# A decode layer with a sliding attention window: one more 64 KB transfer from ScalarE's queue

## The chip, the cores and the metric

The kernel runs on one core of a Trainium2 chip. The metric is the time of one execution in microseconds (us) on the device; lower is better. The time before is 377.72 us, the median of 3 runs (377.6 to 378.23).

A core has five engines with instruction streams of their own: PE (matrix products), DVE and ACT (vector and scalar work), POOL, and SP, which in this kernel only issues transfers. Transfers are carried out by 16 DMA engines, which the queues of SP and ACT share.

## The reference

One decode step (one token for each of 4 sequences) of a transformer layer, in bfloat16: attention over the last 4096 entries of a key-value cache, then a gated feed-forward.

```python
B, Sq, D = 4, 1, 576
Hq, Hkv, Sk, Dh = 32, 16, 16384, 128
W = min(4096, max(256, Sk // 4))                 # 4096
q = (layernorm(x) @ wq)                          # [4, 32 heads, 1, 128]
k = repeat(k_cache[:, :, Sk - W:, :], 2, axis=1) # two query heads share a key head
v = repeat(v_cache[:, :, Sk - W:, :], 2, axis=1)
p = softmax(q k^T * Dh ** -0.5)
h = x + (p v) @ wo
gate, up = layernorm(h) @ W_gate, layernorm(h) @ W_up
out = h + (relu(gate) * up) @ W_down             # F = 4608
```

The keys and values of the window are 2 x 64 MiB, the weights some 25 MB; nothing is used twice from HBM.

## The kernel before

**Order by hand.** A small class `Sched` writes each engine's program one after the other. `S.op` adds an instruction, `S.dma` a transfer; both take a list of names to wait for (`deps`) and may give a name that others wait for. Every engine has one counting semaphore, every key of transfers one of its own, and a wait is a wait on constants. The order in a program is the order on its engine. A transfer counts 16 on its semaphore when it is through; `land(name)` is the name under which its landing is waited for.

**The loads.** `prog_sync` issues all loads but one from SP's queue, in this order: wq's last 64 rows (`("wq", 4)`, 512 KB), its first 512 rows (`("wq", 0)`, 4 MB), then K and V. The attention goes over 16 quads, one for four key heads of one sequence: `quad(cache, i)` gives the window of four heads as 128 partitions (32 to a head) with 32768 contiguous bytes each, 4 MB in all. K0, K1, V0, K2, V1, ... alternate over a pool of four slots in SBUF; each issue waits until the reader of the slot's old content is through (`("TR", ...)` for a K slot, `("PV", i)` for a V slot, `"QMM"` for the two slots that wq lies in at first). Then follow wo, W_gate, W_up and, in six pieces of falling size (`WD`, line 253), W_down. The only other load is x (four rows of 1152 bytes), from ScalarE's queue, line 291.

**The products with wq.** wq's 512 first rows are read as 128 partitions of four rows each and are multiplied with `xnT`, the transposed normalised x. The 64 last rows are read as 128 half rows, and are multiplied with `xn4`, in which each value of x stands on two partitions and `par` keeps the one or the other (lines 307 to 309): the odd products. PE takes these first (`c == 4`, line 483), since their load lands first; they wait for `"XN41"`, the second of the two xn4 copies. The last product is `"QMM"`. After it ACT copies q to `q_bf` (line 311), DVE transposes it into `qT` (line 427, after the first transpose of K0), and PE spreads it (`"QREP"`).

**The attention.** For each quad, four times: DVE transposes a quarter of K in 32-bit units into `kT` (`tr`, line 395; `kT` has NKT = 3 buffers of 2048 float32 on each partition, used in turn), and PE multiplies it with the spread q (`qk`, line 497). The maximum, exponentials, a transpose of the probabilities and the products with V (`pv`, line 515) follow, V of a quad one quad behind its K.

**The end.** wo, the second layer norm, the gated products and W_down, whose pieces PE takes in order as they land; the last product is `"DOWN1"`, after which ACT and DVE copy one part of the output each and SP stores it.

ACT's program around the change, in order: x is issued; small constants; `D_X4`, `D_XNT` (the transposed x from PSUM); `FOE`, `IDF`, `SPOT`, `SAME` (line 305); the two copies `XN40` and `XN41`; the copies of q.

Of the kernel before, what the change touches and what calls it, by code (L numbers as in the profile page):

```python
# [9 lines left out]
BF16 = mybir.dt.bfloat16  # L10
# [91 lines left out]
def bass_sequential_preLN__sliding_block_cached__glu_gated_reglu__decode_kernel(  # L102
# [12 lines left out]
    with ExitStack() as es:  # L115
        cnt = [0]

        def sb(name, shape, dt):
            return es.enter_context(nc.sbuf_tensor(name, shape, dt))

        pool = sb("pool", [128, NSLOT * QUAD], BF16)
        kT = sb("kT", [128, NKT, QUAD // 8], FP32)
# [74 lines left out]
        S = Sched()  # L197
# [56 lines left out]
        for k, (f0, f1) in enumerate(WD):  # L254
            transfers.append((("wd", k), f"wd{k}", ["ATTN"],
                              lambda e, f0=f0, f1=f1: e.dma_start(
                                  out=pool[:, f0 * D:f1 * D], in_=B_W_down.rearrange("(p j) n -> p (j n)", j=JJ)[:, f0 * D:f1 * D])))
# [4 lines left out]
        def land(name):  # L262
            return ("L",) + (name if isinstance(name, tuple) else (name,))
# [25 lines left out]
        def prog_act(S):  # L289
            a = "scalar"  # L290
            S.dma(a, lambda e: e.dma_start(out=x_bf[:, :], in_=A_x.rearrange("b s d -> (b s) d")), "x", name=land("x"))
            S.op(a, lambda e: e.activation(out=st1[:, 14:15], in_=st1[:, 13:14], func=ACT.Sqrt, bias=eps_c[0:B, 0:1], scale=1.0),
                 deps=["D_VAR", "EPS"], name="A_STD")
            S.op(a, lambda e: e.copy(out=dup[:, :].rearrange("p (r u) -> p r u", u=2),
                                     in_=bass.AP(tensor=ident_b, offset=0, ap=[[128, 64], [1, 64], [0, 2]])), deps=["IDB"], name="DUP")
            S.op(a, lambda e: e.copy(out=col[:, :].rearrange("p (a s) -> p a s", s=NS),
                                     in_=bass.AP(tensor=ident_b, offset=0, ap=[[128, NS], [0, 128], [1, NS]])), name="COL")
# [3 lines left out]
                                           in_=bass.AP(tensor=ident_b, offset=0, ap=[[128, NS], [0, 16], [1, NS], [0, 2]]),  # L301
# [2 lines left out]
            S.op(a, lambda e: e.activation(out=spot[:, :], in_=spot[:, :], func=ACT.Copy, scale=-SCALE), deps=["SPOT0"], name="SPOT")  # L304
            S.op(a, lambda e: e.copy(out=same[:, :].rearrange("p (x h) -> p x h", h=NHQ),
                                     in_=bass.AP(tensor=mask, offset=0, ap=[[NHQ, 128], [0, 16], [1, NHQ]])), deps=["M0"], name="SAME")
            for u in range(2):
                S.op(a, lambda e, u=u: e.activation(out=xn4[:, u, 0:B], in_=pb[STB][:, 0:B], func=ACT.Copy, scale=par[:, u:u + 1]),
                     deps=["XDUP", "PAR2", "XN4Z"], name=f"XN4{u}")
            for k in range(2):  # L310
                S.op(a, lambda e, k=k: e.copy(out=q_bf[:, k, :].rearrange("p (x e k) -> p x e k", e=2, k=32),
                                              in_=pb[QB[k]].rearrange("p (x k e) -> p x e k", e=2, k=32)), deps=["QMM"], name=f"QBF{k}")
            S.op(a, lambda e: e.copy(out=qrep[:, :, :].rearrange("p x (g y) -> p x g y", g=4),
                                     in_=sc.ap().rearrange("p (g r) -> p g r", g=4)[:, :, 0:128].rearrange("p g (x y) -> p x g y", x=4)),
                 deps=["QREP"], name="D_QR")
# [16 lines left out]
            for i in range(NQUAD):  # L332
                S.op(a, lambda e, i=i: e.activation(out=diag[:, i % 2, :], in_=spot[:, :], func=ACT.Copy, scale=rmx[:, i % 2:i % 2 + 1]),  # L333
                     deps=[("RMAX", i), "SPOT"], name=("DIAG", i))
                deps = [("BIAS", i)]
                if i >= 2:
                    deps.append(("TRP", i - 2))
                S.op(a, lambda e, i=i: e.activation(  # L338
                    out=Pb[:, (i % 2) * 1024:(i % 2 + 1) * 1024], in_=sc[:, (i % 2) * 1024:(i % 2 + 1) * 1024], func=ACT.Exp,
                    scale=SCALE, bias=bias[:, i % 2:i % 2 + 1], accum_out=rs1[:, i:i + 1]),  # L340
                    deps=deps, name=("EXP", i))
                if i + 2 < NQUAD:
                    qzero(i + 2)
            S.op(a, lambda e: e.copy(out=bass.AP(tensor=spread, offset=0, ap=[[16 * H, H], [4 * H + 1, 4], [4, H]]),
                                     in_=bass.AP(tensor=ident_b, offset=0, ap=[[128, H], [0, 4], [1, H]])),
                 deps=["SP0"], name="SPREAD")
            S.op(a, lambda e: e.copy(out=oX[:, :, :].rearrange("p e b -> p (e b)"), in_=pb[0][:, 0:EO * B]), deps=["OSEL"], name="OX")  # L347
            S.op(a, lambda e: e.activation(out=st2[:, 14:15], in_=st2[:, 13:14], func=ACT.Sqrt, bias=eps_c[0:B, 0:1], scale=1.0),
                 deps=["D_VAR2"], name="A_STD2")
            S.op(a, lambda e: e.copy(out=hnT[0:64, 4, 0:B], in_=tpv[0:64, 16:20]), deps=["TP2", "HN4Z"], name="N1")  # L350
            S.op(a, lambda e: e.copy(out=hnT[:, 0:4, 0:B], in_=tpv[:, 0:16].rearrange("p (c b) -> p c b", b=B)), name="N2")
            for u in range(2):
                S.op(a, lambda e, u=u: e.activation(out=hn4[:, u, 0:B], in_=pb[SUB][:, 400:400 + B], func=ACT.Copy, scale=par[:, u:u + 1]),
                     deps=["HDUP"], name=f"HN4{u}")
            for k, (f0, f1) in enumerate(CUTS):
                S.op(a, lambda e, k=k, f0=f0, f1=f1: e.activation(out=gate_sb[:, :, f0:f1].rearrange("p j f -> p f j"), in_=part(0, k, "f j"), func=ACT.Relu),
                     deps=[("GATE", k)], name=("RELU", k))
# [3 lines left out]
        def prog_dve(S):  # L361
# [12 lines left out]
            for k in range(5):  # L374
                w = 1 << k
                S.op(v, lambda e, w=w: e.tensor_scalar(out=num[:, w:2 * w], in0=num[:, 0:w], scalar1=float(w), scalar2=None, op0=ALU.add),
                     deps=["NUM0"] if k == 0 else [("NUM", k - 1)], name=("NUM", k))
            S.op(v, lambda e: e.transpose(out=numT[:, :], in_=num[:, :]), deps=[("NUM", 4)], name="NUMT")
            for k in range(4):
                S.op(v, lambda e, k=k: e.tensor_tensor(out=ident_b[32 * k:32 * k + 32, 32 * k:32 * k + 32], in0=num[32 * k:32 * k + 32, :],  # L380
                                                       in1=numT[32 * k:32 * k + 32, :], op=ALU.is_equal),
                     deps=["NUMT", "P0"] if k == 0 else [], name="IDB" if k == 3 else None, signal=k == 3)
# [4 lines left out]
                 name="PAR2")  # L387
# [6 lines left out]

            def tr(i, j):
                f = 4 * i + j
                deps = [land(("K", i))]
                if f >= NKT:
                    deps.append(("QK", f - NKT))
                x0 = at[("K", i)] + j * (QUAD // 4)  # L400
                src = pool[:, x0:x0 + QUAD // 4].bitcast(FP32).rearrange("p (t c k) -> p c t k", c=2, k=32)
                dst = kT[:, f % NKT, :].rearrange("p (c t k) -> p c t k", c=2, k=32)
                S.op(v, lambda e: e.transpose(out=dst, in_=src), deps=deps, name=("TR", f))  # L403
# [19 lines left out]
            for i in range(NQUAD):  # L423
                for j in range(4):
                    tr(i, j)
                    if i == 0 and j == 0:
                        S.op(v, lambda e: e.transpose(out=qT[:, :], in_=q_bf[:, :, :].rearrange("p k x -> p (k x)")), deps=["QBF1"], name="D_QT")  # L427
                        S.op(v, lambda e: e.tensor_reduce(out=bass.AP(tensor=gath, offset=0, ap=[[2 * H, 128], [H + 16, 2], [NHQ, 2], [1, NHQ]]),
                                                          in_=bass.AP(tensor=ident_f, offset=0, ap=[[128, 128], [0, 2], [64, 2], [1, NHQ], [NHQ, 8]]),
                                                          axis=AX.X, op=ALU.add), deps=["IDF", "G0"], name="GATH")  # L430
                    if j == 0 and i > 1 and i % 2 == VLEAD:
                        own(i // 2 - 1)
                rmax(i)
                fbias(i)
                trp(i)
# [8 lines left out]
                 deps=["RS", ("EXT", NQUAD // 2 - 1)], name="NORM")  # L444
# [3 lines left out]
            for k, (f0, f1) in enumerate(CUTS):  # L448
                S.op(v, lambda e, k=k, f0=f0, f1=f1: e.tensor_tensor(out=hh[:, :, f0:f1], in0=part(1, k, "j f"), in1=gate_sb[:, :, f0:f1], op=ALU.mult),
                     deps=[("GU", k), ("RELU", k)], name=("HH", k))  # L450
            for j in range(2):
                j0, j1 = j * JJ // 2, (j + 1) * JJ // 2
                S.op(v, lambda e, j0=j0, j1=j1: e.transpose(out=hhT[:, j0:j1, :].rearrange("p j b -> p (j b)"),
                                                            in_=hh[:, j0:j1, :].rearrange("p j f -> p (j f)")),
                     deps=[("HH", len(CUTS) - 1)], name=("HHT", j))
# [3 lines left out]
        def prog_pe(S):  # L459
# [134 lines left out]
            for k, (f0, f1) in enumerate(WD):  # L594
                deps = [land(("wd", k))]
                for f in range(f0, f1):
                    if f % (JJ // 2) == 0:
                        deps = deps + [("HHT", f // (JJ // 2))]
                    for u in range(2):
# [3 lines left out]
                        deps = []  # L603

        progs = [("gpsimd", prog_pool), ("sync", prog_sync), ("scalar", prog_act), ("vector", prog_dve), ("tensor", prog_pe)]
        S.begin(False)
        for _, p in progs:
# [32 lines left out]
```

## Time and profile before

| what | value |
|---|---|
| median of 3 runs | 377.72 us (377.6 to 378.23) |
| the profiled execution | 378.56 us |
| its span, first to last instruction | 377.2 us |
| busy: PE, DVE, ACT, POOL | 80%, 60%, 14%, 1% |
| packets of queue q1 (SP) | 159.59 MB, 98.8% of 16 DMA engines' span |
| K load, issue to landing (median of 16) | 26.8 us |
| V load, issue to landing (median of 16) | 26.4 us |
| chain that ended last | DMA 47%, DVE 29%, PE 20%, ACT 3% |

A busy share is that of one engine over the span. The chain that ended last is followed back from the last instruction, at each step to what released it. A line of a timeline has the start in us, the duration in us, the engine, the line in the code, the operation, what it writes and reads, and in brackets how long the engine had been idle and what ended that. A line of the table of stretches has the stretch, its length, then busy time and (x) instructions of PE, PEld (weight loads), DVE, ACT and POOL, the granted clock of PE, the DMA share and GB/s.

These are the issues from SP's queue that the prediction speaks of, and three around them, from the timeline of that queue:

```profile
1.64 1.25 SPq L226 DMA_DIRECT2D pool<-in_A_k_cache_dram  x2
17.55 0.54 SPq L231 DMA_DIRECT2D pool<-in_A_v_cache_dram  x1
18.13 0.60 SPq L226 DMA_DIRECT2D pool<-in_A_k_cache_dram  x1
...
319.43 0.33 SPq L245 DMA_DIRECT2D pool<-in_A_wo_dram  x1
...
352.45 2.70 SPq L256 DMA_DIRECT2D pool<-in_B_W_down_dram  x6
```

K0 and K1 are issued at 1.64 us, V0 and K2 when wq's slots are free at 17.55, and the six pieces of W_down at 352.45.

### The profile page before, as it was taken

What the parts mean: (1) busy time and instruction counts of PE and PEld (TensorE: products, weight loads), DVE (VectorE), ACT (ScalarE), POOL (GpSimd) and SP (SyncE); (2) the same over time, 40 slices, a digit from 0 to 9 for tenths busy, and PEclk for the clock granted to TensorE, in tenths of its full rate; (3) what the DMA queues carried; (4) which work ended last, traced back from release to release, by engine and by line L of the source; (5) the groups of instructions that cost most, each with busy time, mean ns of one, the idle gap of its engine ahead of it and who ended that gap; (6) DMA issues with size and microseconds to landing.
All of it is one profiled execution on the core that took longest, in us unless ns stands there. A gap on an engine that the chain in (4) does not pass through costs nothing.

```text
span 377.2 us, 2603 instructions
## 1 busy us (share of the span) xinstructions
PE 302.2 (80%) x1432; PEld 73.0 (19%) x772; DVE 225.8 (60%) x165; ACT 53.4 (14%) x140; POOL 5.2 (1%) x15
## 2 busy tenths in 40 slices
PE   0509299969996999499969996899879996968667
PEld 0101022212221222022212221122112121212214
DVE  8046677595849493858476846666675768231230
ACT  2202402110220112002200220020202010101020
POOL 5000000000000000000000000000000000000000
PEclk9999789998999899989989997799959998996988
DMA  8999999999999999999999999999999999999996
GB/s 334 445 445 389 445 440 393 445 440 438 422 424 441 438 434 408 441 441 427 413 440 441 431 427 427 440 434 427 420 441 440 417 424 441 422 432 429 443 404 255
DMA packets 6506, 159.74 MB, mean 423 GB/s; under 512 B 728, under 2 KB 864, under 8 KB 1632
## 3 DMA queue, kind: packets, MB, share of 16 engines
q1 hardware_dynamic: 6488, 159.59, 98.8%
q8 instruction: 8, 0.13, 0.1%
q10 hardware_dynamic: 8, 0.00, 0.0%
q14 instruction: 2, 0.02, 0.0%
HBM read 159.58 MB, written 0.00 MB: 423 GB/s over the span
## 4 chain that ended last, share of the span: by engine, by line
DMA 47%; DVE 29%; PE 20%; ACT 3%; SPq 1%; issue 1%; DVEq 0%
DMA pool<-in_A_k_cache_dram 41%; DVE kT L403 20%; PE sc L466 7%; PE sc L468 6%; DMA pool<-in_B_W_down_dram 5%; DVE acc L420 4%; PE val L466 3%; PE val L468 3%; DVE own_sb L417 2%; DVE probT L414 2%; ACT P L338 2%; PE pb L466 1%; DVE o_bf L442 0%; ACT L338 0%; DVE rmx L406 0%
## 5 line engine op out<-in xcount | busy, mean ns | idle before, releaser
L403 DVE STREAM_TRANSPOSE kT<-pool 128x2048 f32<-128x2048 f32 x64 | 142.8, 2278 | 25.3 <-DMA pool<-in_A_k_cache_dram 24.3
L466 PE MATMUL sc<-kT,qz 128*128 128x512 bf16 x256 | 110.5, 432 | 36.6 <-DVE kT L403 36.3
L468 PE MATMUL sc<-kT,qz 128*128 128x512 bf16 x256 | 109.6, 428 | 0.0
L466 PE MATMUL val<-pool,probT 128*64 128x512 bf16 (+2 forms) x328 | 104.2, 374 | 4.4 <-DMA pool<-in_B_W_down_dram 4.4
L468 PE MATMUL val<-pool,probT 128*64 128x512 bf16 x256 | 96.2, 379 | 0.0
L466 PEld LDWEIGHTS sc<-kT,qz 128*128 128x128 bf16 x256 | 26.7, 104 | 146.5 <-issue 71.1
L466 PEld LDWEIGHTS val<-pool,probT 128*64 128x64 bf16 (+1 forms) x328 | 32.1, 107 | 81.3 <-issue 68.5
L406 DVE TENSOR_REDUCE rmx<-sc 128x1 f32<-128x1024 f32 x16 | 19.6, 1225 | 41.0 <-PE sc L468 41.0
L333 ACT ACTIVATE diag<-spot,rmx 128x16 f32<-128x16 f32 x16 | 4.9, 307 | 234.0 <-DVE rmx L406 234.0
L414 DVE STREAM_TRANSPOSE probT<-P 128x1024 bf16<-128x1024 bf16 x16 | 19.9, 1246 | 21.0 <-ACT P L338 21.0
L338 ACT ACTIVATE P<-sc,bias 128x1024 bf16<-128x1024 f32 x16 | 17.8, 1114 | 21.0 <-DVE bias L409 21.0
L327 ACT COPY qz<-qrep 32x128 bf16<-32x128 bf16 x64 | 18.8, 294 | 0.6
L409 DVE TENSOR_REDUCE bias<-pb 128x1 f32<-128x16 f32 x16 | 2.8, 175 | 23.8 <-PE pb L466 23.8
L420 DVE TENSOR_REDUCE acc<-own_sb 128x128 f32<-128x1024 f32 x8 | 15.2, 1897 | 0.3
L417 DVE TENSOR_TENSOR own_sb<-val,mask 128x1024 f32<-128x1024 f32 x8 | 9.6, 1200 | 7.9 <-PE val L468 7.9
L466 PE MATMUL sc<-pool,oX 128*4 128x288 bf16 x32 | 10.0, 338 | 0.4 <-ACT oX L347 0.4
L468 PE MATMUL sc<-pool,oX 128*4 128x288 bf16 x32 | 9.9, 336 | 0.0
L478 PE MATMUL pb<-ident_b,xn_bf 4*128 4x4 bf16 (+1 forms) x5 | 0.4, 180 | 10.0 <-DVE xn_bf L371 10.0
L466 PE MATMUL sc<-qT,sel 32*128 32x128 bf16 x4 | 0.3, 284 | 9.6 <-DVE qT L427 9.6
L445 DVE TENSOR_TENSOR h_row<-sc,x_bf 4x576 f32<-4x576 f32 x1 | 0.7, 745 | 11.6 <-PE sc L468 11.6
L466 PE MATMUL pb<-diag,same 128*128 128x16 f32 x32 | 6.3, 273 | 1.7 <-ACT diag L333 1.7
L466 PEld LDWEIGHTS pb<-diag,same 128*128 128x128 f32 x32 | 4.8, 188 | 11.8 <-ACT diag L333 7.4
(102 smaller groups left out, 85.7 us busy)
## 6 DMA issues: line engine op xcount, KB each, us to landing
pool<-in_A_k_cache_dram SPq DMA_DIRECT2D x16, 4096.0 KB, 26.8
pool<-in_A_v_cache_dram SPq DMA_DIRECT2D x16, 4096.0 KB, 26.4
pool<-in_A_wo_dram SPq DMA_DIRECT2D x1, 4608.0 KB, 18.3
pool<-in_B_W_gate_dram SPq DMA_DIRECT2D x1, 4608.0 KB, 18.6
pool<-in_B_W_up_dram SPq DMA_DIRECT2D x1, 4608.0 KB, 24.7
pool<-in_A_wq_dram SPq DMA_DIRECT2D x1, 4096.0 KB, 12.7
pool<-in_B_W_down_dram SPq DMA_DIRECT2D x1, 2016.0 KB, 15.0
pool<-in_B_W_down_dram SPq DMA_DIRECT2D x1, 1296.0 KB, 17.7
```

Source lines behind the costliest of these rows:

```text
L327: S.op(a, lambda e, src=src, dst=dst: e.copy(out=dst, in_=src), deps=deps, name=("QZ", i) if g == 3 else None, signal=g == 3)
L333: S.op(a, lambda e, i=i: e.activation(out=diag[:, i % 2, :], in_=spot[:, :], func=ACT.Copy, scale=rmx[:, i % 2:i % 2 + 1]), deps=[("RMAX", ...
L338: S.op(a, lambda e, i=i: e.activation(out=Pb[:, (i % 2) * 1024:(i % 2 + 1) * 1024], in_=sc[:, (i % 2) * 1024:(i % 2 + 1) * 1024], func=ACT ...
L403: S.op(v, lambda e: e.transpose(out=dst, in_=src), deps=deps, name=("TR", f))
L406: S.op(v, lambda e: e.tensor_reduce(out=rmx[:, i % 2:i % 2 + 1], in_=sc[:, (i % 2) * 1024:(i % 2 + 1) * 1024], axis=AX.X, op=ALU.max), dep ...
L409: S.op(v, lambda e: e.tensor_reduce(out=bias[:, i % 2:i % 2 + 1], in_=pb[TPB][:, 16 * (i % 2):16 * (i % 2) + 16], axis=AX.X, op=ALU.min), ...
L414: S.op(v, lambda e: e.transpose(out=pT[i % NPT], in_=Pb[:, (i % 2) * 1024:(i % 2 + 1) * 1024]), deps=[("EXP", i)] + ([("PV", i - NPT)] if ...
L417: S.op(v, lambda e: e.tensor_tensor(out=own_sb[:, :].rearrange("p (x d) -> p x d", d=DH), in0=val[:, :].rearrange("p (x d) -> p x d", d=DH ...
L420: S.op(v, lambda e: e.tensor_reduce(out=acc[:, w % 2, :], in_=own_sb[:, :].rearrange("p (x d) -> p d x", d=DH), axis=AX.X, op=ALU.add), de ...
L445: S.op(v, lambda e: e.tensor_tensor(out=h_row[:, :], in0=attn, in1=x_bf[:, :], op=ALU.add), deps=["ATTN", land("x")], name="H")
L466: return e.matmul(o, lhsT=l, rhs=r, start=start, stop=stop, skip_group_check=skip)
L468: return e.add_instruction(mybir.InstMatmult(name=nc.get_next_instruction_name(), start_tensor_calc=start, stop_tensor_calc=stop, bass_ski ...
```

## The change

ScalarE issues one more transfer, after `SAME` and ahead of the two xn4 copies. It reads the first eight rows of wq as four pieces of two rows (16384 contiguous bytes each) and writes them to partitions 0, 8, 16 and 24 of the first two buffers of `kT`, which nothing has used by then. Nothing reads them. Since DVE's first transpose overwrites the first buffer, it waits for this transfer to land as well as for K0. Everything else stays.

```diff
             S.op(a, lambda e: e.copy(out=same[:, :].rearrange("p (x h) -> p x h", h=NHQ),
                                      in_=bass.AP(tensor=mask, offset=0, ap=[[NHQ, 128], [0, 16], [1, NHQ]])), deps=["M0"], name="SAME")
+            S.dma("scalar", lambda e: e.dma_start(
+                out=kT[0:32:8, 0:2, :].rearrange("p f n -> p (f n)").bitcast(BF16), in_=A_wq[0:8, :].rearrange("(a c) n -> a (c n)", c=2)),
+                "stagger", name=land("stagger"))
             for u in range(2):
                 S.op(a, lambda e, u=u: e.activation(out=xn4[:, u, 0:B], in_=pb[STB][:, 0:B], func=ACT.Copy, scale=par[:, u:u + 1]),
                      deps=["XDUP", "PAR2", "XN4Z"], name=f"XN4{u}")
@@
             def tr(i, j):
                 f = 4 * i + j
-                deps = [land(("K", i))]
+                deps = [land(("K", i))] + ([land("stagger")] if f == 0 else [])
                 if f >= NKT:
                     deps.append(("QK", f - NKT))
```

## Prediction

> **What bounds the kernel now.** I read first the page's DMA rows, then busy time in four stretches, then the end of the timeline, and last the trace's record of every DMA packet (start, duration, bytes, queue, but no engine number).
>
> ```profile
> span 377.2 us, 2603 instructions
> ...
> DMA  8999999999999999999999999999999999999996
> ...
> q1 hardware_dynamic: 6488, 159.59, 98.8%
> q8 instruction: 8, 0.13, 0.1%
> q10 hardware_dynamic: 8, 0.00, 0.0%
> q14 instruction: 2, 0.02, 0.0%
> ```
>
> The 16 DMA engines are busy from end to end: SP's queue q1 alone fills 98.8% of them. PE (80%) and DVE (60%) follow what lands. q10 is ScalarE's queue; its 8 packets are the four rows of x and four semaphore writes, so a transfer with four outer rows runs on four engines. q8 fetches instructions in 8 packets of 16384 bytes.
>
> ```profile
> 3.60:20.00 16.40, 5.27 (x46) 1.18 (x26) 6.03 (x19) 3.29 (x13) 2.11 (x6) 1.00 0.98 422
> 20.00:57.00 37.00, 22.23 (x83) 4.67 (x45) 23.29 (x14) 7.14 (x18) 0.00 (x0) 0.91 1.01 425
> 62.00:97.00 35.00, 31.53 (x133) 7.33 (x69) 24.49 (x16) 5.17 (x14) 0.00 (x0) 0.95 1.00 433
> 101.00:320.00 219.00, 191.19 (x777) 43.40 (x403) 149.39 (x92) 27.36 (x73) 0.00 (x0) 0.92 1.00 432
> ```
>
> The last column is GB/s. Between 20 and 57 us the queues are full and yet move 425 GB/s, later 433. (The first stretch has smaller packets and bins that cut them, so it is not compared.)
>
> ```profile
> 374.00 1.38 PE L466 MATMUL val<-pool,probT 128*4 128x320 bf16 x14 [0.39 <-DMA pool<-in_B_W_down_dram]
> ...
> 375.42 0.41 ACT L358 CAST out_sb<-val 4x320 bf16<-4x320 f32 x1 [13.51 <-PE val L466]
> 375.42 0.42 DVE L456 CAST out_sb<-val 4x256 bf16<-4x256 f32 x1 [9.02 <-PE val L466]
> 375.91 0.33 SPq L269 DMA_DIRECT2D out_dram<-out_sb  x1
> ```
>
> The end hangs on the last piece of W_down: PE waits for it, then about 2.5 us of fixed tail follow. A transfer has landed when the slowest of its 16 engines is through, so the time is set by **the engine that is last at 374.7 us**.
>
> The packet records give that engine. On one engine each packet starts 3 ns before the one before it ends, so the packets link into 16 chains of 405 (45 loads, 8 data packets and a semaphore write each); which chain is which engine the records don't say. A 32768-byte packet takes 1213 ns when undisturbed. Three findings:
> - From 20 to 57 us the mean is 1241 ns, with all chains within 0.4 us of one another and slowed in the same rounds: 479 packets, 0.84 us per engine. From 62 to 97 us the mean is 1215.5 ns. The slowing stops at 57 us, where the first instruction fetch (56.58 us) throws one chain 1.6 us behind the other fifteen.
> - Each of the 8 fetches hits another chain, which stays behind: 1.53 to 1.65 us at the end for seven, 1.96 us for one that was 0.4 us late already. Two more chains, hit by q14's two 8192-byte packets, are 0.63 and 0.93 us behind; six are within 0.28.
> - The chain ahead of all ends at 372.73 us, the last at 374.69, and PE goes on at 374.72.
>
> **The change, part by part.**
>
> ```profile
> 11.10 0.28 ACT L305 COPY same<-mask 128x128 f32<-128x128 f32 x1
> 11.29 0.40 ACT L308 ACTIVATE xn<-sc,par 128x4 bf16<-128x4 f32 x2
> ...
> 13.89 0.62 PE L466 MATMUL val<-pool,xnT 128*32 128x512 bf16 x4 [1.02 <-DMA pool<-in_A_wq_dram]
> ```
>
> *The issue.* One transfer more in ScalarE's queue, between these two ACT rows; the issue of x took 0.55 us there. That moves the two xn copies, and PE's eight odd-product matmuls with them, by at most 0.55 us; they end 1.02 us before wq lands, so half the cover is left. Without cover it would still cost nothing: the q copies end at 18.63 us and the transpose that reads them starts at 25.88. What is queued behind the issue on ACT (q copies, qrep, qz) waits for PE anyway.
>
> *The wait.* The first K transpose (23.64 us) also waits for the new transfer. Issued at 11.4 us, it should land by 16 at the latest (x took 1.2 us from issue to its last row; here a packet of up to 1.4 us stands ahead on each engine). Nothing; behind it on DVE stands all of the attention, which would move by what is late.
>
> *The bytes.* 16384 bytes on each of four engines that are never idle. Nothing later gives that time back: each of these engines runs every following packet later by s. Lower bound of s: half a 32768-byte packet, 0.61 us. Upper bound: the fetches, packets of the same size from another queue, which cost their chains 1.4 to 1.7 us each. The 8192-byte ones cost 0.58 and 0.85 us where their bytes alone would be 0.30, so a change of queue takes 0.28 to 0.55 us on top. 0.61 plus 0.4 is **s = 1.0 us**, taken nearer the plain packets, since it too is an HBM-to-SBUF copy.
>
> Where s shows at the end depends on which chains it falls on. On a chain that no fetch hits (0 to 0.94 us behind), it ends 1.0 to 1.94 behind, not later than today's last: **0**. On one that is hit (1.55 to 1.65), it ends about 2.6 us behind, 0.65 us later than today's last (bounds: 0.2 to 1.4). Following the two late rows of x through the first 2 us, the closest links lead to chains without a fetch, or to a tie between one with and one without, so I lean to the first.
>
> *The rounds between 20 and 57 us.* s comes at about 12.5 us, before they begin, and puts four chains where one chain was put at 57 us. If being in step is the cause, the 0.84 us go, all but the 0.07 or so that the stretch from 62 to 97 us also shows: **-0.75 us** for every chain. Bounds: 0 (the stretch slows for another reason) and -1.1 (the one chain that is 0.4 us late by then is spared too). A loss is bounded by the last rival.
>
> *What is issued earlier or later.* Landings of K move by -0.75 to +1.0 us, and the loads that wait for freed slots move with them. By the packet records a load's first packet starts 5.2 us after its issue at least (wo: issued 319.43, started 324.61), so no engine runs dry.
>
> [...]
>
> **Sum.** 0 (issue) + 0 (wait) + 0 (s on chains with room) - 0.75 (rounds). The profiled execution took 378.56 us, 1.3 more than its span of 377.2; the median of the runs is 377.72, and I put the difference on that: **377.0 us**.
>
> **Rivals.**
> - *Rounds gone, but s falls on a chain that a fetch hits later.* -0.75 + 0.65 = -0.1: 377.6 us. For it: eight of sixteen chains are hit. Against it: the links of x.
> - *In step is not the cause, and s has room.* 377.7 us: a transfer wholly hidden. For it: the slowing began at 20 us in the middle of a load, though the chains had been in step since 13. Against it: its end falls on the very packet at which the first fetch strikes.
> - *In step is not the cause, and s falls on a hit chain.* +0.65: 378.4 us. This is plain added work on a full engine.
> - *The slowing lasts longer.* One mechanism on the other side: the shift is close to a whole packet (1.21 us), so the four chains fall into the same rhythm one packet later, and the fetch at 57 us, which can strike one of these four or leave too many in step, no longer ends the rounds. They would then go on to the next fetch at 97.7 us: 41 us at 0.84 per 37 is +0.9, and with half of the 0.65 for a hit chain +1.2: 378.9 us. It decides if more than about 15 us of further rounds are added. Against it: one chain 1.6 us off was enough before.
> - *It doesn't do what it says* (the pieces spread over 16 engines): 64 KB over 16 is 0.15 us each and no stagger, within the second rival; x's four rows on q10 speak against it.
>
> **Chances.** Forecast 0.44, rivals in order 0.18, 0.06, 0.20, 0.12. About 0.2%, 0.76 us, is what a measurement of this kernel can tell from no change. The forecast sits on that edge: 0.32 of its 0.44 counts as faster, since what can be spared reaches to -1.1, and 0.12 as no change. The first rival gives 0.03, 0.14 and 0.01; the second 0.06 no change; the third 0.06 no change and 0.14 slower; the fourth 0.12 slower. Together faster 0.35, same 0.38, slower 0.27. The range runs from 376.4 (all of the bound -1.1, and the runs' own spread below the median) to 378.9 (the fourth rival). The forecast's own range is 376.4 to 377.4.
>
> **What would show it.** In the changed profile: 20 to 57 us at 432 or 433 GB/s (rounds gone) or at 425 (not); four chains 0.6 to 1.5 us behind from 13 us on; q10 with 16 packets (right) or 40 (spread); the largest lag at the end 1.6 to 1.9 us (room) or 2.2 to 3.3 (hit); K0's first transpose at most 1 us later; wq's products starting up to 1 us later without effect on V0's landing. The prediction fails if the rounds stay, if they last past 57 us, or if s lies far above 1.5 us.

## The result and the profile after

The changed kernel takes 378.4 us (median of 22 runs, 377.95 to 378.58), the kernel before 377.75 us in as many runs beside it (377.56 to 378.42): ratio 1.0015 with a 95% interval of 1.0008 to 1.0021, **0.65 us slower**. 377.0 us was forecast, with 376.4 to 378.9 as the range.

The profiled execution of the changed kernel took 378.58 us. The page's lines on the DMA engines:

```profile
span 377.2 us, 2605 instructions
...
DMA  8999999999999999999999999999999999999995
...
q1 hardware_dynamic: 6488, 159.59, 98.6%
q8 instruction: 8, 0.13, 0.1%
q10 hardware_dynamic: 16, 0.07, 0.0%
q14 instruction: 3, 0.02, 0.0%
```

The span is that of before to the tenth, and ScalarE's queue q10 has the 16 packets that four pieces on four engines give (e6_eight's eight pieces make 24 of them, e4_sixteen's 16 pieces 40; q14's third packet has 80 bytes). The four stretches (busy time of PE, PEld, DVE, ACT, POOL, granted clock, DMA share, GB/s):

```profile
3.60:20.00 16.40, 5.27 (x46) 1.20 (x26) 6.03 (x19) 3.29 (x13) 2.11 (x6) 1.00 0.99 418
20.00:57.00 37.00, 20.98 (x75) 4.20 (x41) 22.07 (x13) 6.84 (x17) 0.00 (x0) 0.72 1.00 429
62.00:97.00 35.00, 31.53 (x132) 7.34 (x69) 25.09 (x16) 3.62 (x10) 0.00 (x0) 0.95 0.99 426
101.00:320.00 219.00, 191.46 (x784) 43.67 (x408) 151.19 (x93) 27.34 (x73) 0.00 (x0) 0.93 1.00 431
```

From 20 to 57 us the rate rose from 425 to 429 GB/s, but from 62 to 97 us it fell from 433 to 426, though the packet records show nothing there: a 32768-byte packet took 1217 ns on average in the first of these stretches and 1219.9 from 57 to 97 us. A packet counts in GB/s where it falls, so the column is good to some 4 GB/s over 35 us (an estimate: four 32768-byte packets more or fewer), and the packet records are the sharper reading. They say that the rounds of 20 to 57 us are gone (1241 ns before).

Timelines: first around the new issue, then the ends.

```profile
10.47 0.68 ACTq L307 DMA_DIRECT2D kT<-in_A_wq_dram  x1
...
11.28 0.40 ACT L311 ACTIVATE xn<-sc,par 128x4 bf16<-128x4 f32 x2
...
14.03 0.62 PE L469 MATMUL val<-pool,xnT 128*32 128x512 bf16 x4 [1.16 <-DMA pool<-in_A_wq_dram]
...
17.69 0.54 SPq L231 DMA_DIRECT2D pool<-in_A_v_cache_dram  x1
...
24.87 2.31 DVE L406 STREAM_TRANSPOSE kT<-pool 128x2048 f32<-128x2048 f32 x1 [14.93 <-DMA pool<-in_A_k_cache_dram]
```

```profile
374.74 0.09 PEld L469 LDWEIGHTS val<-pool,probT 128*4 128x4 bf16 x4 [0.33 <-DMA pool<-in_B_W_down_dram]
...
375.44 0.41 ACT L361 CAST out_sb<-val 4x320 bf16<-4x320 f32 x1 [13.65 <-PE val L469]
375.44 0.42 DVE L459 CAST out_sb<-val 4x256 bf16<-4x256 f32 x1 [8.84 <-PE val L469]
375.93 0.34 SPq L269 DMA_DIRECT2D out_dram<-out_sb  x1
```

ACT's sequencer issues the transfer at 10.47 us, while the engine still works on what stands ahead of it (`SAME` starts at 11.09), and the xn copies stay where they were (11.28, before 11.29). wq's products come 0.14 us later and V0's issue too; K0's first transpose comes 1.23 us later (before 23.64). The end is the same as in the profile of before (375.93, before 375.91), and PE waits for W_down as before.

So the two *profiled* executions are equal, and the *medians* are 0.65 us apart. The packet records, linked into 16 chains as in the prediction, show how (the chains are a reconstruction: where two end within a few ns of one another, a link can be exchanged):

| | before | after |
|---|---|---|
| the chain ahead of all ends at | 372.73 us | 372.04 us |
| the last chain ends at | 374.69 us | 374.68 us |
| lag of the last | 1.96 us | 2.65 us |

The chain ahead gained 0.69 us, and one chain took 0.69 us back. The experiments had to tell which of the two belongs to the median.

### The profile page after: what moved, and what is told of

The parts are those of the page before. It is cut to its first block, busy times and chain, and to the rows that moved or that the text cites. A ratio compares the mean times of both kernels' runs of the same rounds, so it can differ in the third digit from the quotient of the medians.

```text
span 377.2 us, 2605 instructions
## 1 busy us (share of the span) xinstructions
PE 301.3 (80%) x1432; PEld 73.2 (19%) x772; DVE 225.7 (60%) x165; ACT 53.4 (14%) x140; POOL 5.2 (1%) x15
## 3 DMA queue, kind: packets, MB, share of 16 engines
q1 hardware_dynamic: 6488, 159.59, 98.6%
## 4 chain that ended last, share of the span: by engine, by line
DMA 45%; DVE 29%; PE 21%; ACT 3%; issue 0%; SPq 0%; DVEq 0%
DMA pool<-in_A_k_cache_dram 41%; DVE kT L406 20%; PE sc L469 7%; PE sc L471 6%; PE val L469 5%; DMA pool<-in_B_W_down_dram 4%; DVE acc L423 4%; PE val L471 3%; DVE own_sb L420 2%; DVE probT L417 2%; ACT P L341 2%; PE pb L469 1%; DVE o_bf L445 0%; ACT L341 0%; DVE rmx L409 0%
## 5 line engine op out<-in xcount | busy, mean ns | idle before, releaser
L469 PE MATMUL sc<-pool,oX 128*4 128x288 bf16 x32 | 9.2, 319 | 0.4 <-ACT oX L350 0.4
L471 PE MATMUL sc<-pool,oX 128*4 128x288 bf16 x32 | 9.2, 319 | 0.0
## 6 DMA issues: line engine op xcount, KB each, us to landing
pool<-in_B_W_down_dram SPq DMA_DIRECT2D x1, 2016.0 KB, 15.6
```

Source lines behind the costliest of these rows:

```text
L469: return e.matmul(o, lhsT=l, rhs=r, start=start, stop=stop, skip_group_check=skip)
L471: return e.add_instruction(mybir.InstMatmult(name=nc.get_next_instruction_name(), start_tensor_calc=start, stop_tensor_calc=stop, bass_ski ...
```

## The experiments

Apart from three repeats (one profiled execution each), e11_early and e12_balance, each changes only the destination, source or size of the new transfer; "pieces" are its parts, one on each engine that it uses. The table gives each run's ratio to the kernel before of its own batch, and from its one profiled execution the chain that is ahead, the last one, its lag, and what the chains that carry no piece lose in one or two packets while the pieces run (14 to 17 us; a 32768-byte packet over 1213 ns).

| run | pieces, to partitions | ratio (95%) | ahead, last, lag (us) | lost by the others (us) |
|---|---|---|---|---|
| before | none | 1 | 372.73, 374.69, 1.96 | 0 |
| e1_before | none | one run | 372.50, 374.44, 1.94 | 0 |
| e16_before | none | one run | 372.56, 374.49, 1.94 | 0 |
| after | 4 x 16 KB, 0 8 16 24 | 1.0015 (1.0008 to 1.0021) | 372.04, 374.68, 2.65 | 0.14 to 0.16, two 0.46 to 0.50 |
| e8_after | the same | one run | 372.53, 374.49, 1.97 | 0.41 to 0.52 |
| e2_tiny | 4 x 512 B, 0 8 16 24 | 1.0001 (0.9993 to 1.001) | 371.81, 373.75, 1.94 | 0 |
| e3_two | 2 x 16 KB, 0 8 | 1.0000 (0.9991 to 1.0008) | 372.02, 374.00, 1.97 | 0 to 0.1, one 0.41 |
| e7_half | 4 x 8 KB, 0 8 16 24 | 1.0002 (0.9993 to 1.001) | 372.14, 374.06, 1.92 | 0.10 to 0.14, two 0.18 and 0.23 |
| e4_sixteen | 16 x 4 KB, 0 8 ... 120 | 1.0008 (1.0000 to 1.0017) | 372.23, 374.08, 1.86 | none without a piece |
| e6_eight | 8 x 8 KB, 0 8 ... 56 | 1.0009 (1.0001 to 1.0018) | 372.39, 374.21, 1.82 | 0.14 |
| e5_24k | 4 x 24 KB, 0 8 16 24 | 1.0029 (1.0018 to 1.0040) | 372.61, 374.75, 2.14 | 0.58 to 0.79 |
| e9_apart | 4 x 16 KB, 0 8 16 24 | 1.0016 (1.0008 to 1.0025) | 372.52, 374.69, 2.17 | 0.52 to 0.69 |
| e11_early | 4 x 16 KB, 0 8 16 24 | 1.0009 (1.0000 to 1.0018) | 372.47, 374.36, 1.89 | 0.45 to 0.62, before 13.6 us |
| e13_upper | 4 x 16 KB, 64 68 72 76 | 1.0019 (1.0010 to 1.0027) | 372.47, 374.68, 2.21 | 0.48 to 0.60 |
| **e10_dst** | 4 x 16 KB, 0 4 8 12 | 1.0002 (0.9993 to 1.0011) | 371.86, 373.92, 2.06 | 0 to 0.04, one 0.05 |
| e15_own8k | 4 x 8 KB, 0 4 8 12 | 0.9998 (0.9989 to 1.0007) | 371.98, 373.98, 2.00 | 0 |
| e14_own24k | 4 x 24 KB, 0 4 8 12 | 1.0007 (0.9998 to 1.0016) | 371.84, 374.38, 2.54 | 0 |

### First batch: is it the issue, the bytes, or the number of engines?

**e1_before**, the kernel before again, unchanged.

> The kernel before, profiled once more. Theory A (the slowed rounds between 20 and 57 us were a peculiarity of the one profiled execution, which took 378.56 us while 22 runs have a median of 377.75): this execution moves 432 or 433 GB/s between 20 and 57 us, its packets of 32768 bytes take 1217 ns in the mean there, and its span is about 376.4 us; the last chain of packets is 1.6 to 1.9 us behind the first. Theory B (the rounds belong to the kernel before, and the added transfer removes them, but loses as much elsewhere): 425 GB/s and 1241 ns again, span about 377.2 us.

Measured: 378.36 us in its one execution. Neither theory holds as it stands: the rounds are there again, but smaller (1223.7 ns, 0.32 us from 20 to 57 us) and 0.48 us of them lie behind 57 us.

**e2_tiny**, the same issue and wait with 512 bytes to a piece:

```diff
-                out=kT[0:32:8, 0:2, :].rearrange("p f n -> p (f n)").bitcast(BF16), in_=A_wq[0:8, :].rearrange("(a c) n -> a (c n)", c=2)),
+                out=kT[0:32:8, 0, 0:128].bitcast(BF16), in_=A_wq[0:4, 0:256]),
```

> The same transfer to the same four partitions, but with pieces of 512 bytes. Theory A (the loss is the bytes on a chain that ends last): nearly nothing, 0 to +0.3 us on the kernel before. Theory C (the loss is the issue on ScalarE's queue, the wait of the first K transpose, or the switching of queues): +0.5 to +0.7 us, as with 16384 bytes.

377.82 us against 377.81. Two lines of its timeline:

```profile
23.72 2.31 DVE L406 STREAM_TRANSPOSE kT<-pool 128x2048 f32<-128x2048 f32 x1 [13.78 <-DMA pool<-in_A_k_cache_dram]
...
374.98 0.33 SPq L269 DMA_DIRECT2D out_dram<-out_sb  x1
```

K0's first transpose is within 0.08 us of before: issue, wait and change of queue cost nothing; what costs comes with the bytes. This profile has no rounds from 20 to 57 us (1213.6 ns) and ends 0.93 us before the profile of before, yet the median is the same. From this it follows, though no profile of the kernel before shows such an execution, that **most executions of the kernel before have few or no rounds, and that there was next to nothing in the median to win back.**

**e3_two**, two pieces (`kT[0:16:8, 0:2, :]`, four rows of wq), and **e4_sixteen**, the 64 KB spread over 16 pieces of 4096 bytes:

```diff
+                out=kT[0:128:8, 0, 0:1024].bitcast(BF16), in_=A_wq[0:8, :].rearrange("a (c n) -> (a c) n", c=2)),
```

> Two pieces of 16384 bytes in place of four, so two engines of the four. Theory A: if one of the two is the engine that ended last with four pieces, +0.65 us on the kernel before as with four; if not, 0 to +0.3 us. In either case the profile shows which chains carry the pieces and what else they carry. Theory D (the loss grows with the bytes added in all, wherever they fall): half of it, +0.3 us.

> The same 64 KB as sixteen pieces of 4096 bytes, one on each engine. Theory A: every chain is late by its share alone, 0.15 us by the bytes and up to 0.5 us with the change of queue, so +0.15 to +0.5 us on the kernel before, and the spread of the chains stays as in the kernel before (1.6 to 1.9 us, not 2.65). Theory D: +0.65 us.

Two pieces of the full size cost nothing that can be measured (1.0000), 16 small ones 0.20 us, at the edge of its interval. A piece as such is not the price.

### Second batch: size, and a second profile of the change

**e5_24k** (`kT[0:32:8, 0:3, :]`, three rows to a piece), **e7_half** (`kT[0:32:8, 0, :]`, one row) and **e6_eight** (`kT[0:64:8, 0, :]`, eight pieces of one row).

> Four pieces of 24576 bytes in place of 16384. Theory A (the time is set by one chain that carries a piece, an 8192-byte packet of q14 and its own late start): that chain is later by the time of 8192 bytes more, 0.30 us, so +0.95 us on the kernel before; the leading chain still ends at about 372.0 us. Theory B (four chains held back lose time to contention, not to bytes): the same +0.65 us as with 16384.

> [...] This is to show which engines the instruction fetches hit. [...] If some hit chains carry a piece, these end 1.7 + 0.4 = 2.1 us behind the first, and the time is +0.2 to +0.4 us too, so here the profile tells, not the time.

> Four pieces of 8192 bytes. Theory A: the late chain is 0.30 us less late than with 16384, so +0.35 us on the kernel before, and its lag at the end is 2.3 us where it was 2.65. Theory B: +0.65 us, as with 16384.

**e8_after**, the changed kernel again, unchanged.

> The changed kernel, profiled once more. Theory A: the last chain is again one with a piece and an 8192-byte packet of q14, at 2.3 to 2.7 us behind the first; no slowed rounds between 20 and 57 us; the leading chain ends at about 372.0 us. Theory E (the late chain of the first profile was chance, its start late by 0.7 us): the last chain is at most 2.2 us behind, and the time is 378.0 us or less, or something else holds the end.

Time over before, each in its own batch: +0.04 us with 8 KB to a piece, +0.65 with 16 KB, +1.05 with 24 KB. 8 KB was expected to cost +0.35 at least and does not; 24 KB costs a little more than the +0.95 of theory A. e6_eight is 0.35 us slower, inside its 0.2 to 0.4, and six of the eight fetches fall on its eight chains without a piece. The second profile of the changed kernel tells more: its last chain is an ordinary one that a fetch hit, with a lag of 1.97 us, and the late chain of the first profile is missing. Its end in the timeline:

```profile
373.84 1.36 PE L469 MATMUL val<-pool,probT 128*4 128x320 bf16 x14 [0.41 <-DMA pool<-in_B_W_down_dram]
...
375.74 0.35 SPq L269 DMA_DIRECT2D out_dram<-out_sb  x1
```

It is as slow as the first all the same (378.38 us): here **all 16 chains** are late, and theory A is refuted. Beside e2_tiny, the chain ahead is 0.72 us later and the lag 0.03 larger; in the first profile of the change it was 0.23 and 0.71. The prediction had no term for what happens to a chain that carries no piece.

### Third batch: what slows the chains that carry nothing?

**e9_apart** takes the four sources 1.2 MB apart (`in_=A_wq.rearrange("(a r) n -> a (r n)", a=4)[:, 0:2 * H * DH]`), **e11_early** issues the same transfer right behind x, before any packet of K0 runs, and **e10_dst** moves nothing but the destination:

```diff
-                out=kT[0:32:8, 0:2, :].rearrange("p f n -> p (f n)").bitcast(BF16), in_=...
+                out=kT[0:16:4, 0:2, :].rearrange("p f n -> p (f n)").bitcast(BF16), in_=...
```

> The four pieces read from four places 1.2 MB apart, in place of 64 KB in a row. In two profiles of the changed kernel all twelve chains without a piece lost 0.14 and 0.43 us while the pieces ran. Theory F (this stall comes from the source: four engines on one stretch of HBM): the twelve lose under 0.1 us, and the time is +0.2 to +0.4 us on the kernel before. Theory G (it comes from the bytes or from the destination): they lose 0.14 to 0.43 us again, and the time is +0.55 to +0.7 us.

> The pieces go to partitions 0, 4, 8 and 12 in place of 0, 8, 16 and 24. Theory H (the stall comes from the destination, since a piece writes where another engine is writing): with other partitions it changes, under 0.1 us for the twelve chains, and the time is +0.2 to +0.4 us on the kernel before. Theory F or a stall by the bytes alone: as in the changed kernel, 0.14 to 0.43 us and +0.55 to +0.7 us.

> The same transfer as in the changed kernel, issued right behind x, at about 1.3 us, while the engines begin with wq. Theory A (bytes on a chain that a packet of q14 hits too): +0.55 to +0.7 us on the kernel before, wherever the pieces lie in time. Theory I (the stall of all chains costs most, and it needs the pieces to meet K0's packets of 32768 bytes): the twelve chains without a piece lose under 0.1 us; the four are 0.6 to 0.9 us late, which leaves most of them room; +0.1 to +0.4 us.

The source is not it: 0.60 us slower with the sources apart, and the others lose 0.52 to 0.69 us. Nor does it need packets of K0 beside it: issued early, the pieces start between 5.8 and 7.4 us, the chains without a piece lose 0.45 to 0.62 us by 13.6 us, and the kernel is 0.42 us slower, which lies between what the two theories gave. The destination is it: on partitions 0, 4, 8 and 12 the cost is gone (377.88 us, as before), and with it the 0.2 to 0.4 us that theory H had left for the bytes. From the packet records, the 32768-byte packets of some chains from 11.5 us on, each as ns over 1213, and the pieces in brackets (ns, start in us):

```
after (partitions 0, 8, 16, 24)
 0 2 0 143 1 0 0 9 0 1
 0 0 0 493 11 0 5 3 8 0
 0 0 0 145 0 2 5 8 3 0
 0 0 0 147 0 2 8 3 3 9
 0 0 [q10 611@14.8] 429 0 6 3 0 2 11
 0 0 0 [q10 676@15.5] 102 5 0 5 0 11
e10_dst (partitions 0, 4, 8, 12)
 0 0 5 7 14 0 13 3 0 0 0
 0 0 0 0 0 8 8 0 0 0
 0 33 2 0 0 21 0 0 0 0
 0 0 [q10 611@14.7] 0 0 0 0 0 0 0
 0 0 [q10 611@14.7] 0 0 0 0 0 0 0
 0 0 105 [q10 611@15.6] 0 0 14 0 0 0 0
```

In the upper half one packet of every chain is lengthened by 102 ns or more, the chains without a piece too (of the chains not shown, one has its delay in two packets, 83 and 75 ns). In the lower half the pieces take their 611 ns. Beside them run one packet with 105 ns more (14.2 to 15.6 us, on the chain whose own piece comes last) and, on a chain not shown, one with 53; the other packets that run beside them take at most 14 ns more (the one with 33 ends as the first pieces begin). The timeline of e10_dst:

```profile
10.68 0.68 ACTq L307 DMA_DIRECT2D kT<-in_A_wq_dram  x1
...
24.26 2.31 DVE L406 STREAM_TRANSPOSE kT<-pool 128x2048 f32<-128x2048 f32 x1 [14.12 <-DMA pool<-in_A_k_cache_dram]
...
373.29 1.35 PE L469 MATMUL val<-pool,probT 128*4 128x320 bf16 x14 [0.41 <-DMA pool<-in_B_W_down_dram]
...
375.17 0.35 SPq L269 DMA_DIRECT2D out_dram<-out_sb  x1
```

K0 lands 0.62 us later than before, one piece's 611 ns; with the change it was 1.23, the piece and the stall. The store leaves 0.76 us earlier than with the change.

**e12_balance** was a try at something else: the kernel before, with W_down's third piece divided by partitions into transfers of 112, 6, 6 and 4, to take bytes off some engines at the end.

```diff
+        PARTS = {2: ((0, 112), (112, 118), (118, 124), (124, 128))}
...
+            for r, (p0, p1) in enumerate(PARTS.get(k, ((0, 128),))):
...
+                                      out=pool[p0:p1, f0 * D:f1 * D], in_=...[p0:p1, f0 * D:f1 * D])))
```

> [...] -0.25 us on the kernel before, and the last chain 0.2 us less behind. [...]

382.51 us, 1.0125 (1.0111 to 1.0139): 4.6 us slower, where the expectation failed. The DMA issue of the 112 partitions, and the end of its timeline:

```profile
pool<-in_B_W_down_dram SPq DMA_DIRECT2D x1, 756.0 KB, 24.2
```

```profile
376.06 1.23 PE L468 MATMUL val<-pool,probT 128*4 128x320 bf16 x9 [2.79 <-DMA pool<-in_B_W_down_dram]
```

It lands 24.2 us after its issue (the undivided 864 KB before: 19.3), and PE stands 2.79 us for it. Its 6912-byte packets took 534 ns on average, 262 before. Why is not shown: no record tells which engine writes which rows, and three more issues and three small transfers changed as well.

### Fourth batch: which destinations?

**e13_upper** keeps e10_dst's spacing of four partitions, 64 further up (`kT[64:80:4, 0:2, :]`): if the spacing made the difference it should be free (0 to +0.1 us), if it is which partitions are written, it can stall as the change does (+0.5 to +0.7 us, an estimate from the change's +0.65). **e14_own24k** and **e15_own8k** are e10_dst with 24 KB and 8 KB to a piece (`kT[0:16:4, 0:3, :]` and `kT[0:16:4, 0, :]`), where only the bytes on the four engines remain.

> Four pieces of 16384 bytes to partitions 64, 68, 72 and 76, four apart as in the run without a stall, but in the upper half. [...]

> Four pieces of 24576 bytes to partitions 0, 4, 8 and 12. Theory H: no stall, the twelve others lose under 0.05 us; what is left is the bytes on the four chains, 0.9 us each, and the chain that a packet of q14 hits too ends 0.5 + 0.9 + 1.0 = 2.4 us behind, 0.4 later than the last hit chain: +0.2 to +0.45 us on the kernel before, against +1.05 with partitions 0, 8, 16, 24. If bytes and not the destination made the loss: +1.05 us.

> Four pieces of 8192 bytes to partitions 0, 4, 8 and 12: the one that could beat both kernels, if 0.3 us of delay on four chains keeps the slowed rounds away at no price. Theory H: no stall, the four chains end at most 1.9 us behind, as the hit ones do; 0 on the kernel before, down to -0.15 us if the rounds go in every execution.

> The kernel before, profiled a third time. If slowed rounds come and go between executions: a mean packet of 1213 to 1241 ns between 20 and 57 us, and a time that goes with it, 377.6 us without rounds and 378.5 us with 0.84 us of them.

e13_upper is 0.74 us slower, a little more than the 0.5 to 0.7: it is not the spacing. Its end beside that of e14_own24k:

```profile
375.44 0.42 DVE L459 CAST out_sb<-val 4x256 bf16<-4x256 f32 x1 [8.83 <-PE val L469]
375.92 0.33 SPq L269 DMA_DIRECT2D out_dram<-out_sb  x1
```

```profile
375.14 0.41 DVE L459 CAST out_sb<-val 4x256 bf16<-4x256 f32 x1 [7.23 <-PE val L469]
375.62 0.35 SPq L269 DMA_DIRECT2D out_dram<-out_sb  x1
```

Half as many bytes again on partitions 0, 4, 8 and 12 cost 0.33 us, within the 0.2 to 0.45 expected, and less than the change does. The chain ahead is where e2_tiny has it (371.84); one chain ends last: 0.49 us late at the start, 1.41 after its 912-ns piece, 2.46 after one of q14's packets, 2.54 at the end. With 8 KB nothing is left (-0.04 us). e16_before, the third profile of the kernel before, took 378.40 us with 0.16 us of rounds from 20 to 57 us and 0.58 from 57 to 97.

None of the versions was faster than the kernel before by more than its interval.

## Why the prediction was wrong

**The step that failed first: "the bytes".** It priced the new packets on the four engines that carry them alone. The missing term is the stall of all 16 chains while pieces are written to partitions 0, 8, 16 and 24. Beside e2_tiny the chain ahead ends 0.23 us (after) and 0.72 us (e8_after) later, 0.71 and 0.66 in e9_apart and e13_upper, and 0.05 in e10_dst. Not all of that is the stall: on the mean of the four chains that carry neither a piece nor a fetch, e8_after is 0.71 us later than e2_tiny, of which 0.39 arise up to 20 us, while 0.19 are there before K0 begins and 0.12 come from 20 to 57 us. The lengthened packets are therefore the surer sign. That the destination decides is shown: between the changed kernel and e10_dst nothing else differs, and e9_apart, beside e10_dst in one batch, is as slow as the change. Of the 1.4 us between 377.0 and 378.4, the destination makes about 0.65; the other 0.75 is the second step below.

Why these partitions? No run shows it. The records give neither engine numbers nor the partitions that a packet writes, so theory H's reason, that a piece writes where another engine is writing, is an idea that nothing here confirms. That it is the same four engines whatever the partitions is likely: in all six profiles with four pieces of 16 KB q14's two 8192-byte packets fall on two of the four, and the eight fetches on none. What is measured is the cost by destination (0.00 us to partitions 0, 4, 8 and 12, +0.65 to 0, 8, 16 and 24, +0.74 to 64, 68, 72 and 76) and that in the two slow cases the chains without a piece are held up too (0.14 to 0.69 us); what holds them is not shown.

**The second: "-0.75 us".** The size was there in the profile: with the change the chain ahead ends 0.69 us earlier and the mean packet from 20 to 57 us fell from 1241 to 1217 ns. But the saving was put on a median that does not contain it. Three profiled executions of the kernel before took 378.36 to 378.56 us, its median is 377.72 to 377.88 over the batches; e2_tiny's profiled execution without rounds took 377.61. The prediction noted that the profiled execution was 0.84 us above the median, nearly the size of the saving, and did not ask whether it was the same thing. Nor do the rounds need chains set apart by 1 us to go: e2_tiny's pieces take 27 ns, and it has none from 20 to 57 us. In the three profiles of before the rounds lie in different places (0.98, 0.80 and 0.74 us from 20 to 97 us), and e12_balance, whose program is that of before until W_down, has 0.31 us of them. Why all three profiled executions of before had that many stays open; so does whether being in step is their cause. So does a smaller one: from 20 to 57 us the mean packet took 1216.9 to 1217.2 ns in seven profiles with four pieces of 8 KB or more to partitions 0, 8, 16, 24 or 64 to 76, but 1213.1 to 1213.8 ns in e2_tiny and the three runs with partitions 0, 4, 8, 12; that is 0.1 us more of the loss.

**s on chains with room: the size was near, but not for its reason, and the room half right.** s was put at 1.0 us between 0.61 and 1.4 to 1.7. The pieces set their four chains 0.59 to 0.85 us further behind the chain ahead, and without a stall a piece took its 611 ns and set its chain back by 0.57 to 0.6 (e10_dst): the lower bound, without the 0.4 us that were added for the change of queue. No fetch hit one of the four chains in any of the six profiles with four pieces of 16 KB, as the lean to x's chains had it. But the two 8192-byte packets of q14, booked as 0.63 and 0.93 us on chains of their own, fall among the same four. In the first profile of the change one chain collected all: 0.70 us late at the start, 1.55 after its piece, 2.56 after q14's packet, 2.65 at the end, which was the last of all. In the second the same sum ended at 1.82, below the fetch-hit 1.97. Over the six profiles with four pieces of 16 KB the lag of the last chain is 1.89 to 2.21 us with this one exception, where before has 1.94 to 1.96: "0" was low by up to 0.27, and by 0.7 in one. At 24 KB on partitions 0, 4, 8 and 12 it shows by itself (e14_own24k, +0.33).

**Issue and wait at 0: right**, by e2_tiny. The issue ran 0.9 us earlier than booked (10.47 instead of 11.4), so the xn copies did not even move; the pieces started 3.8 to 5 us after it (14.3 to 15.5 us), with two or three more 32768-byte packets of q1 ahead of them in the chains shown, and not by about 12.5 us. K0's transpose was 1.23 us later where at most 1 was allowed; the excess is the stall. **No engine ran dry: right**; SP's issues moved by 0.14 us at V0.

**The rivals.** The third gave 378.4 us, the time measured, but that is luck: its mechanism was s on a chain hit by a fetch, which did not happen. The fourth, longer rounds, did not happen, and the second, hidden altogether, is what e10_dst shows for other partitions. The prediction's signs read as set down: 16 packets of q10 (right), rounds gone by the packet records (as forecast, but the median did not gain by it), lag 2.65 (the "hit" reading, for q14's packet instead of a fetch).

## What to carry to other kernels

Where all DMA engines are full, as here (98.6% of their span by q1 alone), do not price a small extra transfer by its bytes alone: the same 64 KB cost 0.65 us to one set of partitions and nothing that can be measured to another (1.0002). Try other destination partitions before explaining the cost by queues, waits or sources. Before a saving is read from a profile, compare that execution's own time with the median: a slowing that only the profiled execution has cannot be won. And follow the chain that ends last through all its packets, the 8 KB ones of other queues included, since on the late chain here the delays added up and were not paid back (0.70, 1.55, 2.56, 2.65 us).

## What the hardware showed beyond that

- 64 KB to partitions 0, 8, 16 and 24, or to 64, 68, 72 and 76, delayed each of the engines without a piece by 0.14 to 0.69 us; the same 64 KB to partitions 0, 4, 8 and 12 delayed them by 0.05 us at most. It is not linear: to 0, 8, 16 and 24, 32 KB cost 0.04 us in the median, 96 KB 1.05.
- Slow rounds of all chains, about 2% over tens of us, differ between executions of one program in place and size (0.98, 0.80 and 0.74 us in three).
- In the six profiles with four pieces of 16 KB, the eight fetches of q8 struck eight of the 12 chains without a piece, and q14's two 8192-byte packets struck two of the four with one.
